# Operand splitting spread over more steps in a spectral FNet plus token-mixing MLP kernel

## The chip, the cores and the metric

The kernel runs on one core of one Trainium2 chip. The metric is the device time of one execution in microseconds (us): the median over several runs. A run is profiled besides, and its trace gives, for each instruction, its engine, source line, start and length.

The engines that matter here are TensorE (matrix products into PSUM; in the profile PE, its weight loads PEld), VectorE (DVE), ScalarE (ACT), GpSimd (POOL) and SyncE (SP). The last two only issue DMA transfers here: SP issues loads, POOL issues stores, most of them accumulating ones, which add to what already lies in DRAM.

## The reference

`x` has 2048 tokens (sequence) by 640 channels, in fp32. The output is the sum of `x` and of two branches that both take the layer-normalized `x`.

```python
xn = _layernorm(x)
# branch A: FNet; Cr, Ci are 2048 x 2048, Hr, Hi are 640 x 640 DFT matrices
a = xn @ Hr.T
b = xn @ Hi.T
A = Cr @ a - Ci @ b
# branch B: token mixer, w1 2048 x 1728, w2 1728 x 2048
h = _layernorm(xn)
u = gelu(h.T @ w1 + b1)          # 640 x 1728
B = (u @ w2 + b2).T              # 2048 x 640
out = x + A + B
```

## The kernel before

**Precision.** Each fp32 operand is cut in two: a high part, which ScalarE makes by a copy to the type fp32r (`high`, L110), and a low part, which VectorE makes by subtracting the high part (`low`, L113). A product is then three matmuls (`three`, L121 to L123): high by high, high by low, low by high. A low part always waits for its own high part.

**Fewer products.** All large products use a Strassen-like scheme: of 2 x 2 blocks, seven products of sums of blocks in place of eight. So VectorE also makes sums and differences of operand blocks (`sub`, L116, and the first sum of a row, L654). In the seven-product stages the results of the products are added up where they can be: several products accumulate in one PSUM bank, the bank is read out after each of them, and the reads build up the result in SBUF (a first read by ScalarE, L699; a later one by VectorE, which adds the bank to the tile, L693).

**Steps and turns.** The whole program is one list of steps. A step is one operand (the weights side: cut into high and low by `cut_piece`) and the matmuls that take it. `turn_of(i, ...)` issues, in program order, everything that belongs to turn i: DMA loads, sums, reads of PSUM, the high part of the operand of step i + 2 (`AHEAD` = 2; three buffers), further sums (`extras`), entries of `timed`, a number of jobs, the low part of the operand of step i + 2, more jobs, and last the matmuls of step i. Each engine runs its own instructions in this order; an instruction that waits holds up all that is behind it on its engine. The order is written by hand in this way, no scheduler moves it.

**Jobs.** The other operand of the products (`moving`) is the same for all rows of a stage and is prepared during the stage before, in small jobs from a list, of which each turn takes the next one or two (`do_jobs`). `moving_of` (L535) cuts one group q of such an operand (128 partitions, two rows of 640) into the seven operands of the scheme: four high parts on ScalarE, three of them of two pieces at once, as many low parts on VectorE, and three sums there, the first of two pieces. It returns a first job and four more, which stand as one-element tuples: after a tuple job, a turn takes no further job, and a turn called with `short` takes no tuple job at all.

**The stages,** in order of the steps:

- *Columns*: steps 0 to 15 (`first_columns`), then seven groups of 32 steps (`columns(g, h, c)`, L443): the DFT over the sequence. h is the half of the sequence that is summed over (the first three groups after the first columns have h = 0, the last four h = 1), c one of four column blocks of 512. A step has nine matmuls of 512 columns where a fifth row block rides along, else six, or three where only that block is computed. The results C11, C12, C21, C22 (two tiles each) and the fifth rows F0, F1 are read out of PSUM at their own turns, by `fresh` (ScalarE copies the bank into a new tile `c`, L510) or `more` (VectorE adds the bank to that tile, L517), and stored by POOL (`store_y`; L401 adds to DRAM where h is 1) into `y_part`. Six tiles `c` are taken in turn (`c_tile`). Of the turns in a group, those in `JOBS_AT` take a job; in the second half (from `s_half`, step 112) these jobs are first those for the five channel DFT matrices (`matrices(q)`, L602), which negate a row on ScalarE (L606) and run `moving_of`.
- *Hidden* (from `s_hid`, step 240): eight rows of seven steps, the DFT over the channels with `y_part` as weights.
- *Up 0* and *up 1* (from `s_up`, step 296): 2 x 7 rows of seven steps, w1 with the normalized sequence rows. `rows_again` fetches two rows of x, scales them on ScalarE (`normalize`, L212) and runs `moving_of`. Up 1 adds what up 0 stored, applies gelu on ScalarE, and the result is cut for the down stages (row groups 0 to 3 at once, the others go through DRAM in `part_up` and come back by `hidden_rows`).
- *Down 0* and *down 1* (from `s_down`, step 394): 2 x 8 rows of seven steps, w2 with the gelu results; down 1 runs over the other row groups.

The rows of hidden, up and down all come from `row_steps` (L641). Its seven steps are the products 1, 5, 6, 2, 7, 3, 4, in this order; reads come one turn after their product, so product 7's read stands in the sixth turn. `loads_of` and `sums_of` (L659 to L665) say at which turn, counted from the row's first step, blocks are loaded and summed. `early` holds for rows of 512 columns of weights or fewer (up and down), and not for hidden.

**How many jobs a turn takes** is set in the last loop (L878 to L887). In up and down, `LONG_AT` lists for each stage the turns of a period that may take a tuple job; the rest are `short`:

```python
LONG_AT = (
    ((1, 3, 6, 8, 10, 13, 15, 17), 21), ((1, 3, 6, 8, 10, 11, 13), 14), ((1, 3, 4), 7),
)
```

Of the kernel before, what the change touches and what calls it, by code (L numbers as in the profile page):

```python
# [23 lines left out]
NF2 = NFB // 2  # L24
# [24 lines left out]
    ((1, 3, 6, 8, 10, 13, 15, 17), 21), ((1, 3, 6, 8, 10, 11, 13), 14), ((1, 3, 4), 7),  # L49
# [4 lines left out]
def fnet_plus_mixer(  # L54
# [60 lines left out]
    def sub(to, a, b):  # L115
        nc.vector.tensor_sub(to, a, b)  # L116
# [273 lines left out]
    c_turn = [3]  # L390
# [52 lines left out]
    def columns(g, h, c):  # L443
# [71 lines left out]
        def more(name, at, key, e, then):  # L515
            def run():
                nc.vector.tensor_add(cs[name, e], banks[key, e], cs[name, e])  # L517
                store_y(h, *then, cs[name, e])
            reads[s0 + at].append(run)

        for e in range(2):
            fresh("C11", 4, "z", e)
            more("C11", 11 + e, "w", e, (0, c, e))
            fresh("C22", 16, "y", e)
            fresh("C12", 20, "z", e)
            more("C12", 28 + e, "y", e, (1, c, e))
            more("C22", 26 + e, "z", e, (1, c, 2 + e))
            fresh("C21", 32, "z", e, (0, c, 2 + e))
# [6 lines left out]
    def moving_of(stage, q, tag, v):  # L535
# [13 lines left out]
        def hi(i, src, n=1):  # L549
            high(moving[stage, q][:, 0, slice(i, i + n) if n > 1 else i, :], src)  # L550
# [6 lines left out]
        def job1():  # L557
            lo(0, piece(0, 0))

            of = v().rearrange("p m (n d) -> p (m n) d", n=2)  # L560
            sub(of[:, 0:2, :], of[:, 1:4:2, :], of[:, 0:2, :])
            hi(3, both(0), 2)

        def job2():
            lo(1, both(1), 2)
            sub(piece(1, 1), piece(1, 1), piece(0, 0))

        def job3():
            lo(3, both(0), 2)
            sub(piece(1, 0), piece(1, 0), piece(1, 1))  # L570
            hi(5, both(1), 2)

        def job4():
            lo(5, both(1), 2)

        return [job0] + [(f,) for f in (job1, job2, job3, job4)]
# [46 lines left out]
    def hidden_rows(q, at):  # L623
        get, _, rest = from_place(at, lambda v: nc.sync.dma_start(v, part_up[4 + q]), [], "down1", q, f"slab{q}")
        return [get] + [None] * 3 + rest
# [15 lines left out]
    def row_steps(stage, nq, load_piece, at, end, bias=(None, None), base=None, earliest=0, each=None):  # L641
# [9 lines left out]
        def first_sum():  # L651
# [9 lines left out]
        sums_of = {  # L661
            -2 if early else -1: (first_sum,),
            0: (lambda: sub(raw["s"], raw["s"], raw["A11"]), lambda: sub(raw["A21"], raw["A11"], raw["A21"])),
            2: (lambda: sub(raw["A12"], raw["A12"], raw["s"]),),
        }  # L665
# [62 lines left out]
    def up(stage, r, at):  # L728
# [3 lines left out]
        def end(c):  # L732
# [17 lines left out]
            timed[e + 5].append(lambda: gelu(0))  # L750
            timed[e + 6].append(lambda: gelu(1))
            if r < 4:
                timed[e + 6].append(lambda: jobs.extend(moving_of("down0", r, f"slab{4 + r}", lambda: c)))
            else:
                timed[e + 7].append(lambda: nc.gpsimd.dma_start(part_up[r], c))

        s0 = row_steps(f"up{stage}", 4, load_piece, at, end)
# [54 lines left out]
    for q in range(4):  # L812
        get, changes, rest = rows_again(0, q, "v")
        timed[s_hid + 4].append(lambda js=[get, None, None] + changes + rest: jobs.extend(js))
# [16 lines left out]
    for q in range(3):  # L831
        timed[s_down + 14 + 7 * q].append(lambda q=q: jobs.extend(hidden_rows(q, ("x0", "v")[q % 2])))
# [44 lines left out]
    with tc.manual_schedule():  # L877
        for i in range(by_hand, len(steps) + 1):  # L878
            n_jobs = (1, i < BLOCK)
            if BLOCK <= i < s_hid - 6:  # L880
                n_jobs = [(i - BLOCK) % GROUP in at for at in JOBS_AT[i >= s_half]]
            short = False
            if i >= s_up:
                at, of = LONG_AT[min((i - s_up) // (7 * NF2), 2)]
                short = (i - s_up) % of not in at
                n_jobs = (1 + (not short), 0)
# [42 lines left out]
```

## Time and profile before

| what | us |
|---|---|
| median of 3 runs | 896.01 |
| lowest and highest of them | 895.9, 896.72 |
| the profiled execution, whole | 896.53 |
| its span in the trace | 894.6 |

The profiled execution is one more run; its span is the time from its first to its last instruction, and the other 1.9 us lie around it. The clock that TensorE was granted is nine tenths or more in each of the 40 slices of the span. How the views that follow are read:

- The page gives, for each engine, its busy time, the share of the span, and the number of instructions. A line of shares follows the chain of work that ended last back through the program.
- A row of the stretches has: start and end in us from the span's start, length; busy time and count (in brackets) of TensorE's matmuls, its weight loads, VectorE, ScalarE and GpSimd; the granted clock of TensorE (1.00 is full); the busy share of the DMA engines; GB/s.
- A row of the timeline has: start, the time from its start to its end (for xN, of N instructions together) in us, engine, line and operation, tile written <- tiles read, sizes; and in square brackets the idle time of the engine just before, with what ended it.
- A row of waits has: the waiting engine, its tile and line <- what ended the wait; us in all, times, the longest.
- A group of instructions has: line, engine, operation, tiles, count | busy us, mean ns of one | idle us just before them, and what ended it.
- A row of DMA issues has: tile written <- read, queue, count, KB each, median us from issue to landing.

### The profile page before, as it was taken

The numbers are of one execution on the slowest core, as the hardware profiler recorded it, in microseconds if no ns is written. First come the engines' busy times: TensorE is split into PE (matmuls) and PEld (weight loads), VectorE is DVE, ScalarE is ACT, GpSimd is POOL, SyncE is SP. The second block draws the span as 40 slices with busy tenths as digits, with TensorE's granted clock in tenths as the row PEclk, the third lists the DMA queues.
The fourth block names the chain that finished last, engine by engine and source line by source line (L and its number), as shares of the span: only waits on it lengthen the run. The fifth ranks groups of instructions, "written<-read, shape, count | busy, mean of one in ns | idle before, by whom it ended". The sixth has DMA issues, their size and how long they took to land.

```text
span 894.6 us, 13967 instructions
## 1 busy us (share of the span) xinstructions
PE 880.5 (98%) x4964; PEld 798.5 (89%) x4964; DVE 714.8 (80%) x1199; ACT 521.0 (58%) x935; POOL 107.8 (12%) x148
## 2 busy tenths in 40 slices
PE   8999999999999999999999999999999999999998
PEld 5888888888888888888999999999989999999998
DVE  8577888785888888588887867888789877887776
ACT  6446576754666564555555645665576655555553
POOL 0110010101121111112100101000000011111111
PEclk9999999999999999999999999999999999999999
DMA  8941554619284655639576765544545787756875
GB/s 293 320 150 60 175 213 128 237 62 359 38 242 65 176 109 172 151 61 185 126 169 152 163 148 159 198 150 142 143 102 140 184 200 179 171 125 133 162 181 107
DMA packets 82951, 143.81 MB, mean 161 GB/s; under 512 B 8129, under 2 KB 33217, under 8 KB 82625
## 3 DMA queue, kind: packets, MB, share of 16 engines
q1 hardware_dynamic: 64848, 95.72, 33.3%
q0 software_dynamic: 18032, 47.20, 27.0%
q8 instruction: 39, 0.64, 0.3%
q14 instruction: 32, 0.25, 0.1%
HBM read 99.63 MB, written 48.50 MB: 166 GB/s over the span
## 4 chain that ended last, share of the span: by engine, by line
PE 88%; DVE 7%; ACT 2%; issue 2%; DMA 1%; SPq 0%; DVEq 0%; ACTq 0%
PE psum L121 29%; PE psum L123 29%; PE psum L122 29%; DVE piece L113 2%; ACT piece L110 1%; DVE sdown L113 1%; DVE pieces L654 1%; DMA pieces<-y 1%; DVE pair L693 1%; DMA pieces<-in_dft_seq 1%; DVE pair L116 0%; DVE st L165 0%; DVE pairs L116 0%; DVE pieces L116 0%; ACT sdown L110 0%
## 5 line engine op out<-in xcount | busy, mean ns | idle before, releaser
L110 ACT ACTIVATE piece<-pieces 128x512 fp32r<-128x512 f32 (+2 forms) x506 | 317.7, 629 | 244.6 <-PE psum L123 142.5
L113 DVE TENSOR_TENSOR piece<-pieces,piece 128x512 fp32r<-128x512 f32 (+2 forms) x506 | 347.8, 689 | 137.7 <-ACT piece L110 128.6
L121 PE MATMUL psum<-piece,n 128*128 128x512 f32 x584 | 228.4, 391 | 2.5 <-ACT n L110 2.5
L122 PE MATMUL psum<-piece,n 128*128 128x512 f32 x584 | 228.5, 391 | 0.2 <-DVE piece L113 0.2
L123 PE MATMUL psum<-piece,n 128*128 128x512 f32 x584 | 227.4, 391 | 0.0
L121 PEld LDWEIGHTS psum<-piece,n 128*128 128x128 f32 x584 | 109.6, 188 | 27.1 <-ACT n L110 3.8
L122 PEld LDWEIGHTS psum<-piece,n 128*128 128x128 f32 x584 | 109.7, 188 | 26.1 <-DVE piece L113 2.6
L123 PEld LDWEIGHTS psum<-piece,n 128*128 128x128 f32 x584 | 109.7, 188 | 23.2
L121 PE MATMUL psum<-sup,piece 128*128 128x320 f32 x392 | 121.5, 310 | 2.2 <-DVE pair L693 1.6
L121 PE MATMUL psum<-sdown,piece 128*128 128x320 f32 x392 | 121.2, 309 | 1.9 <-DVE pair L693 1.7
L123 PE MATMUL psum<-sup,piece 128*128 128x320 f32 x392 | 121.4, 310 | 0.9 <-DVE piece L113 0.9
L123 PE MATMUL psum<-sdown,piece 128*128 128x320 f32 x392 | 121.1, 309 | 0.0
L122 PE MATMUL psum<-sdown,piece 128*128 128x320 f32 x392 | 121.0, 309 | 0.0
L122 PE MATMUL psum<-sup,piece 128*128 128x320 f32 x392 | 121.0, 309 | 0.0
L116 DVE TENSOR_TENSOR pieces<-pieces 128x512 f32<-128x512 f32 (+3 forms) x142 | 109.6, 794 | 2.6
L121 PE MATMUL psum<-shid,piece 128*128 128x320 f32 x280 | 87.0, 311 | 1.2 <-ACT pair L699 1.2
L123 PE MATMUL psum<-shid,piece 128*128 128x320 f32 x280 | 86.8, 310 | 0.3 <-DVE piece L113 0.3
L122 PE MATMUL psum<-shid,piece 128*128 128x320 f32 x280 | 86.5, 309 | 0.0
L121 PEld LDWEIGHTS psum<-sup,piece 128*128 128x128 f32 x392 | 73.6, 188 | 3.5 <-ACT pair L741 1.4
L121 PEld LDWEIGHTS psum<-sdown,piece 128*128 128x128 f32 x392 | 73.6, 188 | 2.6 <-issue 1.8
L123 PEld LDWEIGHTS psum<-sup,piece 128*128 128x128 f32 x392 | 73.6, 188 | 1.4 <-DVE piece L113 1.1
L122 PEld LDWEIGHTS psum<-sup,piece 128*128 128x128 f32 x392 | 73.6, 188 | 0.0
(93 smaller groups left out, 966.1 us busy)
## 6 DMA issues: line engine op xcount, KB each, us to landing
pieces<-in_dft_seq SPq DMA_DIRECT2D x128, 256.0 KB, 5.1
pieces<-in_w SPq DMA_DIRECT2D x88, 256.0 KB, 3.0
y<-c POOLq DMA_DIRECT2D x80, 256.0 KB, 6.0
out<-pair POOLq DMA_DIRECT2D x38, 320.0 KB, 5.7
pieces<-y SPq DMA_DIRECT2D x32, 320.0 KB, 4.9
pieces<-in_w SPq DMA_DIRECT2D x32, 192.0 KB, 2.9
out<-in_x SPq DMA_DIRECT2D x16, 320.0 KB, 6.9
up<-pair POOLq DMA_DIRECT2D x8, 640.0 KB, 4.0
```

The lines of the kernel that those rows point to most:

```text
L110: nc.scalar.activation(hi, src, AF.Copy)
L113: nc.vector.tensor_sub(lo, src, hi.bitcast(F32))
L116: nc.vector.tensor_sub(to, a, b)
L121: nc.tensor.matmul(psum, wh, mh, start=first, stop=False, skip_group_check=True)
L122: nc.tensor.matmul(psum, wh, ml, start=False, stop=False, skip_group_check=True)
L123: nc.tensor.matmul(psum, wl, mh, start=False, stop=last, skip_group_check=True)
L654: nc.vector.tensor_add(raw["s"], raw["A21"], raw["A22"])
L693: nc.vector.tensor_add(c, b, c)
```

## The change

It has the following parts.

1. *The jobs of `moving_of`.* The high parts leave the jobs with the sums and become jobs of their own, without a tuple: job 0 (high parts of the first pieces), job 1 in a tuple (a low part and a sum), job 2 (high part), job 3 and job 4 in tuples (low part and sum, each), job 5 (high part), job 6 in a tuple (low part).
2. *Jobs for each turn.* From `s_half` on a turn that takes jobs takes up to two, all of them ahead of the low part of its operand. As a tuple job ends the taking, these two are mostly a high part and the tuple job behind it. Hidden, where each turn took one job before, gets a list of its own in `LONG_AT`: turns 0, 1, 4 and 5 of seven may take a tuple job, the others are `short`. Up and down already had two jobs in a turn that isn't `short` and one in a `short` one, and keep that.
3. *Last column group* (`g == 2 * NC - 2`). C12 and C22 are no longer read twice into one tile with a VectorE add: both reads are ScalarE copies into tiles of their own, and both are stored with accumulation in DRAM. That is four VectorE adds less, four ScalarE copies and four POOL stores more. The turn of the six `c` tiles starts at another place (`c_turn`), so that it comes out right at the end.
4. *Sums of `row_steps`.* In hidden the sum for A21 moves from turn 0 of a row to turn 2, that for A12 from 2 to 3. Up and down keep their turns. With the sums their operands' slots of `raws` come free later.
5. *Up 1.* The two gelus of a row move from five and six turns behind its last step to six and seven; the jobs that cut the row for down 0, and the store of the other rows, to eight. The loads of the first row of up come at `s_up - 4` at the earliest.
6. *Fetches.* The fetch of the first sequence rows for up 0 is put on the job list at turn `s_hid - 1` in place of `s_hid + 4`. The row groups that down 1 takes back from DRAM are fetched by two jobs at `s_down + 7` and `s_down + 9` and one in the list, in place of each at the head of its own jobs at `s_down + 14`, `+ 21` and `+ 28`, and their other jobs all follow from `s_down + 14`.

```diff
 LONG_AT = (
-    ((1, 3, 6, 8, 10, 13, 15, 17), 21), ((1, 3, 6, 8, 10, 11, 13), 14), ((1, 3, 4), 7),
+    ((0, 1, 4, 5), 7), ((1, 3, 6, 8, 10, 13, 15, 17), 21), ((1, 3, 6, 8, 10, 11, 13), 14), ((1, 3, 4), 7),
 )
...
-    c_turn = [3]
+    c_turn = [5]
...
         def more(name, at, key, e, then):
+            if g == 2 * NC - 2 and name != "C11":
+
+                return fresh(name, at, key, e, then)
+
...
-            fresh("C22", 16, "y", e)
-            fresh("C12", 20, "z", e)
+            last = g == 2 * NC - 2
+            fresh("C22", 16, "y", e, (1, c, 2 + e) if last else None)
+            fresh("C12", 20, "z", e, (1, c, e) if last else None)
...
             sub(of[:, 0:2, :], of[:, 1:4:2, :], of[:, 0:2, :])
+
+        def job2():
             hi(3, both(0), 2)
 
-        def job2():
+        def job3():
             lo(1, both(1), 2)
             sub(piece(1, 1), piece(1, 1), piece(0, 0))
 
-        def job3():
+        def job4():
             lo(3, both(0), 2)
             sub(piece(1, 0), piece(1, 0), piece(1, 1))
+
+        def job5():
             hi(5, both(1), 2)
 
-        def job4():
+        def job6():
             lo(5, both(1), 2)
 
-        return [job0] + [(f,) for f in (job1, job2, job3, job4)]
+        return [job0, (job1,), job2, (job3,), (job4,), job5, (job6,)]
...
-        get, _, rest = from_place(at, lambda v: nc.sync.dma_start(v, part_up[4 + q]), [], "down1", q, f"slab{q}")
-        return [get] + [None] * 3 + rest
+        return from_place(at, lambda v: nc.sync.dma_start(v, part_up[4 + q]), [], "down1", q, f"slab{q}")
...
-        sums_of = {
-            -2 if early else -1: (first_sum,),
-            0: (lambda: sub(raw["s"], raw["s"], raw["A11"]), lambda: sub(raw["A21"], raw["A11"], raw["A21"])),
-            2: (lambda: sub(raw["A12"], raw["A12"], raw["s"]),),
-        }
+        sums_of = defaultdict(list)
+        sums_of[-2 if early else -1].append(first_sum)
+        sums_of[0].append(lambda: sub(raw["s"], raw["s"], raw["A11"]))
+        sums_of[0 if early else 2].append(lambda: sub(raw["A21"], raw["A11"], raw["A21"]))
+        sums_of[2 if early else 3].append(lambda: sub(raw["A12"], raw["A12"], raw["s"]))
...
-            timed[e + 5].append(lambda: gelu(0))
-            timed[e + 6].append(lambda: gelu(1))
+            timed[e + 6].append(lambda: gelu(0))
+            timed[e + 7].append(lambda: gelu(1))
             if r < 4:
-                timed[e + 6].append(lambda: jobs.extend(moving_of("down0", r, f"slab{4 + r}", lambda: c)))
+                timed[e + 8].append(lambda: jobs.extend(moving_of("down0", r, f"slab{4 + r}", lambda: c)))
             else:
-                timed[e + 7].append(lambda: nc.gpsimd.dma_start(part_up[r], c))
-
-        s0 = row_steps(f"up{stage}", 4, load_piece, at, end)
+                timed[e + 8].append(lambda: nc.gpsimd.dma_start(part_up[r], c))
+
+        s0 = row_steps(f"up{stage}", 4, load_piece, at, end, earliest=s_up - 4)
...
-        timed[s_hid + 4].append(lambda js=[get, None, None] + changes + rest: jobs.extend(js))
+        timed[s_hid - 1].append(lambda js=[get, None, None] + changes + rest: jobs.extend(js))
...
-    for q in range(3):
-        timed[s_down + 14 + 7 * q].append(lambda q=q: jobs.extend(hidden_rows(q, ("x0", "v")[q % 2])))
+    gets_hid, _, rests_hid = zip(*(hidden_rows(q, ("x0", "v")[q % 2]) for q in range(3)))
+    for q in range(2):
+        timed[s_down + 7 + 2 * q].append(lambda q=q: jobs.append(gets_hid[q]))
+    timed[s_down + 14].append(lambda: jobs.extend(rests_hid[0] + [gets_hid[2]] + rests_hid[1] + rests_hid[2]))
...
-            n_jobs = (1, i < BLOCK)
+            n_jobs, short = (1, i < BLOCK), False
             if BLOCK <= i < s_hid - 6:
                 n_jobs = [(i - BLOCK) % GROUP in at for at in JOBS_AT[i >= s_half]]
-            short = False
-            if i >= s_up:
-                at, of = LONG_AT[min((i - s_up) // (7 * NF2), 2)]
-                short = (i - s_up) % of not in at
-                n_jobs = (1 + (not short), 0)
+            elif i >= s_hid:
+                k = sum(i >= s for s in (s_up, s_up + 7 * NF2, s_down))
+                at, of = LONG_AT[k]
+                short = (i - (s_up if k else s_hid)) % of not in at
+            if i >= s_half:
+                n_jobs = (2 * n_jobs[0] - short, 0)
```

## The prediction

> **What bounds the kernel now.** I read the page first, then busy time by stretches of time cut at the stage borders, then what TensorE waited for.
>
> ```profile
> span 894.6 us, 13967 instructions
> PE 880.5 (98%) x4964; PEld 798.5 (89%) x4964; DVE 714.8 (80%) x1199; ACT 521.0 (58%) x935; POOL 107.8 (12%) x148
> ...
> PE 88%; DVE 7%; ACT 2%; issue 2%; DMA 1%; SPq 0%; DVEq 0%; ACTq 0%
> ```
>
> TensorE is the bound: the change touches no matmul, so it can only win or lose the short holes between matmuls. The stretches show where these are (start:end, length, then per engine busy time and count; PE comes first, the clock is the 1.00 near the end).
>
> ```profile
> 213.29:361.82 148.53, 148.53 (x649) 121.67 (x648) 120.68 (x176) 87.82 (x148) 25.22 (x30) 1.00 0.61 156
> 361.82:411.79 49.97, 49.79 (x218) 40.30 (x216) 37.05 (x53) 27.41 (x46) 8.13 (x10) 1.00 0.56 111
> 411.79:538.30 126.51, 124.97 (x842) 123.32 (x841) 100.38 (x144) 69.91 (x116) 14.99 (x18) 1.00 0.68 152
> 538.30:625.51 87.21, 86.58 (x590) 86.22 (x589) 74.37 (x125) 52.83 (x98) 4.09 (x7) 1.00 0.53 167
> 625.51:715.62 90.11, 87.67 (x591) 86.25 (x589) 77.74 (x130) 59.57 (x107) 6.28 (x8) 1.00 0.56 141
> 715.62:816.75 101.13, 99.24 (x675) 98.54 (x673) 81.61 (x134) 56.65 (x102) 15.31 (x19) 1.00 0.70 164
> 816.75:890.83 74.08, 74.08 (x506) 73.81 (x504) 56.78 (x112) 38.64 (x83) 12.88 (x16) 1.00 0.73 152
> ```
>
> A row also counts one to three matmuls that cross its edge; the code gives 504 in the last stage, which has no hole: 74.08 / 504 = 0.147 us for a 320-column matmul. A 512-column one comes every 0.227 us (six from 247.64 to 249.00 in the rows further down). So the holes are length minus count times pitch: the three column groups 648 x 0.227, hole 1.4; the last group 216, 0.9; the channel DFT (hidden) 840 x 0.147, 3.0; up 0 and up 1 588 each, 0.8 and 3.7; down 0 672, 2.35. Together 12.2 us; all but the first 1.4, 10.8 us, lie in stages that the change wants to help, and that caps its gain at 1.2%.
>
> ```profile
> PE psum L121 <- DVE pair L693: 3.3, 5, 1.6
> ...
> PE psum L121 <- ACT pair L699: 1.2, 2, 0.7
> ```
>
> These waits of TensorE (us, times, longest) say which wait ends last: mostly not the operand, but the read of a product out of PSUM on VectorE (L693), without which the next product cannot be added to that bank. In a row of steps VectorE must read product 7 during the sixth step, and in the up and down stages the next row's first sum stands ahead of that read.
>
> **The part that costs: a high part and its low part in one step.** Today a job is one turn. From the second half of the columns on, a turn now takes two: job 0 (high parts on ScalarE) and job 1 (their low part and a sum on VectorE) fall into the same turn, and VectorE's low part of the step's own operand stands behind them. The nearest rows are matrix 0 in the columns (ScalarE, VectorE, TensorE):
>
> ```profile
> 244.22 0.62 ACT L110 ACTIVATE piece<-pieces 128x512 fp32r<-128x512 f32 x1
> 244.74 0.73 ACT L606 ACTIVATE hids<-hids 128x640 f32<-128x640 f32 x1
> 245.37 1.09 ACT L110 ACTIVATE shid<-hids 128x320 fp32r<-128x320 f32 x2
> 270.53 1.31 ACT L510 ACTIVATE c<-psum 128x512 f32<-128x512 f32 x2 [0.76 <-PE psum L123]
> ...
> 245.86 0.49 DVE L113 TENSOR_TENSOR shid<-hids,shid 128x320 fp32r<-128x320 f32 x1 [0.29 <-ACT shid L110]
> 246.39 0.82 DVE L116 TENSOR_TENSOR hids<-hids 128x640 f32<-128x640 f32 x1
> 247.13 0.69 DVE L113 TENSOR_TENSOR piece<-pieces,piece 128x512 fp32r<-128x512 f32 x1
> 247.73 1.22 DVE L116 TENSOR_TENSOR pieces<-pieces 128x1024 f32<-128x1024 f32 x1
> ...
> 247.64 0.39 PE L121 MATMUL psum<-piece,n 128*128 128x512 f32 x1
> 249.00 0.39 PE L121 MATMUL psum<-piece,n 128*128 128x512 f32 x1
> 273.81 0.39 PE L121 MATMUL psum<-piece,n 128*128 128x512 f32 x1
> ```
>
> On ScalarE the operand's high part starts at 244.22, the negation 0.52 later, the first high part at 245.37; its low part starts at 245.86, the sum 0.53 and the operand's low part 1.27 after that. In the kernel before the operand at 247.13 is the next step's, due by 249.23 (its second matmul). In the changed order it is the one due by 247.64 + 0.23 = 247.87, and it ends at 247.82: just in time. But the low part (0.85 to the next) and sum (0.41) of the next turn now push the following operand to 249.75, 0.5 late, and the one after (behind a sum of 1.22) by 0.4. Matrix 0: 0.9. Matrix 1 starts a turn with two copies out of PSUM and loses 0.3. Matrix 2 is the bad place: its turn holds steps of 2.04 and 0.68 (9 and 3 matmuls), so the operand is due at 273.81 + 0.23 plus that 0.3. There the copies can start at 271.15 and end two spacings of 0.48 later, the operand's high part follows, the negation at 272.65, the first high part ends at 273.74, and by the distances above the operand's low part ends at 275.8: 1.4 late. The 1.22 sum of the same group is then late by another 0.9. Matrix 3 has longer steps: 0.2. Columns in all: +3.7 (bounds: 2.3 if only matrix 2 loses; 9.2 if each cost its 2.3).
>
> In the down stage the kernel before already has this pairing once; it made the largest hole of the run:
>
> ```profile
> 746.67 1.08 ACT L110 ACTIVATE sdown<-pairs 128x320 fp32r<-128x320 f32 x2
> ...
> 747.17 0.49 DVE L113 TENSOR_TENSOR sdown<-pairs,sdown 128x320 fp32r<-128x320 f32 x1 [1.43 <-ACT sdown L110]
> 747.69 0.82 DVE L116 TENSOR_TENSOR pairs<-pairs 128x640 f32<-128x640 f32 x1
> 749.04 0.48 DVE L693 TENSOR_TENSOR pair<-psum,pair 128x320 f32<-128x320 f32 x1
> 749.44 0.82 DVE L113 TENSOR_TENSOR sdown<-pairs,sdown 128x640 fp32r<-128x640 f32 x1
> 750.70 0.69 DVE L113 TENSOR_TENSOR piece<-pieces,piece 128x512 fp32r<-128x512 f32 x1
> 751.30 0.68 DVE L654 TENSOR_TENSOR pieces<-pieces 128x512 f32<-128x512 f32 x1
> 751.90 0.48 DVE L693 TENSOR_TENSOR pair<-psum,pair 128x320 f32<-128x320 f32 x1
> ...
> 752.53 0.38 PE L121 MATMUL psum<-sdown,piece 128*128 128x320 f32 x1 [1.56 <-DVE pair L693]
> ```
>
> VectorE idles 1.43 for the high part in the fourth step of a row, has a read, a low part and a sum in the fifth, and then the first sum and the read that TensorE waits for. The changed order moves row group 0 clear of this (0.2 left), puts group 1 into the same two steps (1.75 again), and starts group 2 in the fifth step, where I work out 0.8 by the same distances, and 0.6 for its last low part. Down 0: 3.35 instead of 2.35, +1.0 (bounds -2.3, all hidden, and +2.9, three full ones).
>
> **The parts that pay.** *Up 1.* Gelu and the split of its row come one and two steps later, and the third high part no longer holds ScalarE up in the same turn. By the same distances the first row group still delays its row's read by 1.2, the next two by 0.3 and 0.15, where 3.5 of the hole's 3.7 was: -1.8 (bounds -3.5 and 0). *Up 0.* One pairing stays in the fourth step, without the third high part: 0.4 of 0.8 stays, -0.4. *Hidden.* The kernel before splits a row group on consecutive turns together with two sums (0.82 each) of one step:
>
> ```profile
> 468.62 5.55 DMA pieces<-y
> ...
> 511.32 0.43 ACT pair L699
> ```
>
> VectorE is then about two steps' slack behind; a slot comes free late, its load lands late (5.55), and ScalarE's copy (L699) is late for TensorE. With jobs in four of seven steps and the sums at their own steps, VectorE's work per step is at most 2.6 against 15 x 0.147 = 2.2 and falls below it at once. I take all 1.7 us of these holes as gone (bounds -1.7 and 0). What moves with it: the sum for A21 goes two steps down, so the slot of A11 comes free 4.4 us later; from there to the next row's first sum are four steps, 8.8 us, for a load of 4.9 (below). If VectorE ran two steps late there, that load would be the wait.
>
> *Border of the columns and hidden.* Four VectorE adds of the last group become ScalarE copies (two take 1.31 above), and four stores more go through POOL. VectorE's backlog there made holes of 1.75 (0.5 in the last group, 1.25 in hidden). In the changed order the low parts of matrix 4 again wait for high parts of their own turn, and ScalarE has four copies more: I get operands late by 0.45 and 0.25 and a read late by 0.2, and 0.3 for what follows: -0.55 (bounds -1.75 and +2). The 0.3 is for the fetch of the first sequence rows, moved up to the border: it waits until matrix 4 leaves its buffer (410.2 by my sums), lands 4.0 later, and the scaling on ScalarE, with the read behind it, starts at 415.2, half a us after that.
>
> ```profile
> pieces<-y SPq DMA_DIRECT2D x32, 320.0 KB, 4.9
> ...
> pair<-in_x SPq DMA_DIRECT2D x14, 320.0 KB, 4.0
> ...
> y<-c POOLq DMA_DIRECT2D x80, 256.0 KB, 6.0
> ```
>
> ```profile
> L401 POOL DMA_DIRECT2D y<-c x40 | 34.4, 935 | 167.8 <-DVE c L517 155.7 <-ACT c L510 11.7 <-issue 0.5
> ```
>
> *Costed at nothing.* The four stores: 4 x 0.94 on an engine that is 12% busy; each adds to a place stored eight to ten steps (over 11 us) before and landed after 6.0; without that distance it would hold the hidden loads. The down rows' fetches, now up to eight steps ahead; the first up load, one step later but still two steps (4.4) ahead of its use; the buffer of the down rows' store, a step later.
>
> **Sum**, against the profiled execution (896.53 with what lies around the span): +3.7 + 1.0 - 1.8 - 0.4 - 1.7 - 0.55 = +0.25, 896.8. That execution is 0.5 above the median 896.01, so on the scale of the runs I say 896.3: no change.
>
> **Rivals.** *Faster: the reads are not late.* If VectorE reaches the fifth step a us earlier than I think, up 1 loses 0.3 and down 0 1.3, and 3.4 us more are won: 892.9. For it: two later row groups of the kernel before do the same work there and lose only some 0.3 each. Against it: the 1.43 us of idleness above comes with the pairing. *Slower: the pairing costs its worst in every column group.* If all four matrices cost 2.3, it is 5.5 more: 901.8. It decides at two steps: a chain from PSUM copies to the operand's low part of 4.3 us is harmless between steps of 2.04 (4.08 + 0.23) and not between 2.04 and 0.68. The order puts only one there, which speaks against it. *Slower: the first sequence rows land late.* At 5.55, as the load above, instead of 4.0, ScalarE and the read behind it are 1.05 later than put in; with the operand behind that read 2 us: 898.3. From 4.7 on it costs. *Slower: the stores.* If POOL could issue none while VectorE runs without a gap,
>
> ```profile
> 403.19 0.60 DVE c L517
> ...
> 409.45 0.41 DVE pair L116
> ```
>
> the three stores ahead of the first hidden result would go out at about 410, take 3 x 0.94 and 6.0, and land at 419, 3 us after ScalarE needs their tile: 899.3. Against it: under that gapless stretch the mean issue of 0.94 is no longer than elsewhere. The Trainium skill, "SBUF — State Buffer", section "SBUF: two separate sides", has this mechanism: VectorE instructions in a two-port mode keep GpSimd from writing a DMA's descriptors, 3100 ns in place of 620. By that the four stores would take five times 0.94; the trace's 0.94 disagrees, so the chance by this rule is small. *The change does not do what it says* holds in one point already: with two jobs a turn, the first and the last high parts are not a step ahead of their low parts.
>
> **Chances.** No change 0.42; faster by late reads gone 0.28; slower 0.30, of which the columns 0.13, the landing 0.14, the stores 0.03. About 0.2%, 1.8 us, is what a measurement here can tell from no change. The bounds above, taken as independent, give some 2.6 us to either side (893.7 to 898.9); I stretch that to take in the rivals at 892.9, 898.3 and 899.3 and leave out the one at 901.8 and what is faster still: 892.8 to 899.4. The middle case alone reaches 894.2 to 897.8.
>
> **What would show it.** Right: the stretch of the three column groups is about 152, with TensorE waiting for VectorE's low part (L113) at three places; hidden falls to some 124; up 1 to 88.3; down 0 is 102, with the largest hole behind the read of the second row group. Wrong: columns still 148.5 (then faster by 3.5), down 0 under 100, or a load of sequence rows in TensorE's waits.

## The result, and the profile after

| | kernel before | changed kernel |
|---|---|---|
| median, us | 896.04 | 900.87 |
| lowest to highest | 895.64 to 896.72 | 900.08 to 901.77 |
| profiled execution, us | 896.53 | 900.08 |
| span in the trace, us | 894.6 | 897.9 |

The ratio of the times is 1.0053, with a 95% interval of 1.004 to 1.0066: the changed kernel is slower by half a per cent. The forecast was no change at 896.3, with a range up to 899.4.

The page of the changed kernel first: its span, and instructions and busy time of the engines.

```profile
span 897.9 us, 13990 instructions
PE 883.2 (98%) x4964; PEld 798.0 (89%) x4964; DVE 709.9 (79%) x1195; ACT 522.0 (58%) x939; POOL 111.5 (12%) x152
```

As the diff says, VectorE has four instructions fewer, ScalarE four more, GpSimd four more, TensorE as many as before. The longer span is therefore again holes between matmuls. The same stretches as before, cut at the starts of the same matmuls (columns as in the rows of the prediction):

```profile
212.65:365.24 152.59, 150.43 (x650) 121.13 (x649) 119.69 (x176) 87.48 (x148) 25.22 (x30) 1.00 0.59 153
365.24:415.44 50.20, 50.11 (x217) 40.32 (x216) 35.96 (x50) 29.23 (x50) 12.10 (x14) 1.00 0.70 128
415.44:540.87 125.43, 124.78 (x841) 123.19 (x840) 97.21 (x143) 69.69 (x116) 14.65 (x17) 1.00 0.65 154
540.87:627.67 86.80, 86.59 (x591) 86.22 (x589) 74.77 (x125) 53.09 (x98) 4.09 (x7) 1.00 0.51 167
627.67:718.24 90.57, 88.00 (x590) 86.25 (x589) 77.84 (x130) 58.34 (x106) 6.30 (x8) 1.00 0.53 140
718.24:820.36 102.12, 99.43 (x675) 98.57 (x674) 81.56 (x134) 57.47 (x103) 15.32 (x19) 1.00 0.66 162
820.36:894.44 74.08, 74.08 (x506) 73.81 (x504) 56.77 (x112) 38.66 (x83) 12.88 (x16) 1.00 0.72 152
```

Length against length: the three column groups +4.06, the last group +0.23, hidden -1.08, up 0 -0.41, up 1 +0.46, down 0 +0.99, down 1 nothing; +4.2 us together. The span grew by 3.3 only, since in this execution TensorE's first step began 0.5 us earlier, the stages before the first of these rows took 0.2 less, and 0.35 less passed behind the last matmul. Of what the prediction would take as signs of being right, two came: 152.6 us for the three column groups and 102.1 for down 0. Two didn't: up 1 took 90.6 in place of 88.3, longer than before, and hidden 125.4 in place of some 124.

### The profile page after: what moved, and what is told of

Its sections match the earlier page's. It is cut to its first block, busy times and chain, and to the rows that moved or that the text cites. A ratio compares the mean times of both kernels' runs of the same rounds, so it can differ in the third digit from the quotient of the medians.

```text
span 897.9 us, 13990 instructions
## 1 busy us (share of the span) xinstructions
PE 883.2 (98%) x4964; PEld 798.0 (89%) x4964; DVE 709.9 (79%) x1195; ACT 522.0 (58%) x939; POOL 111.5 (12%) x152
## 4 chain that ended last, share of the span: by engine, by line
PE 86%; DVE 7%; ACT 3%; issue 2%; DMA 2%; SPq 0%; DVEq 0%; ACTq 0%
PE psum L122 29%; PE psum L121 29%; PE psum L123 28%; DVE piece L113 3%; DMA pieces<-in_dft_seq 1%; ACT piece L110 1%; DVE pieces L116 1%; DVE shid L113 1%; DVE sdown L113 1%; DVE pieces L662 0%; DVE pair L701 0%; DVE pair L116 0%; DVE st L165 0%; ACT sdown L110 0%; DVE pairs L701 0%
```

## The experiments

In all runs but the repeat and the combinations a part of the changed kernel is undone or altered. A hole is a step's time from its first matmul to the next step's, less its matmuls at 0.227 or 0.147 us. By the pairing I mean a high part and the low part made from it in the same turn. Where a run leaves a stage as it is in the changed kernel, the stage has the same length within 0.2 us in all these traces, except hidden and up 0; so the stretches tell more here than the medians, which are given as ratios to the kernel before, run beside them.

**The columns, without the pairing.** The edit gives the channel DFT matrices their old five jobs, one to a turn:

```diff
+        if stage == "hid":
+            return [job0] + [(lambda fs=fs: [f() for f in fs],) for fs in ((job1, job2), (job3,), (job4, job5), (job6,))]
...
-            if i >= s_half:
+            if i >= s_hid:
                 n_jobs = (2 * n_jobs[0] - short, 0)
```

> The changed kernel, but in the columns the matrices are cut as before: high part, low part and sum in the old five jobs, one job to a turn; all else stays changed. Theory (a high part and the low part behind it in one turn cost TensorE the holes): the three column groups from step 112 on, 152.6 us in the changed kernel, fall back to 148.5, and the whole to 900.9 - 4.05 = 896.8. Rival (the columns' holes only move the backlog from the border into the groups): 148.5 in the groups, but 2 us or more come back in the steps 234 to 250, the whole 899 or more.

The ratio was 1.0018 (1.0008 to 1.0028); in its trace the three groups and the last one:

```profile
213.40:361.89 148.49, 148.49 (x649) 121.68 (x648) 120.68 (x176) 87.83 (x148) 25.17 (x30) 1.00 0.61 158
361.89:411.39 49.50, 49.50 (x217) 40.56 (x216) 35.41 (x49) 29.23 (x50) 12.07 (x14) 1.00 0.72 129
```

The 4.1 us are gone, and the last group did not pay for them: it is 0.7 shorter too. The steps 234 to 250, where the rival wanted 2 us more, have 1.8 us of holes in place of 2.1, so the rival falls. What the pairing does can be read off the changed kernel's own timeline, at the place that the prediction called the bad one: VectorE, then TensorE.

```profile
274.16 0.49 DVE L113 TENSOR_TENSOR shid<-hids,shid 128x320 fp32r<-128x320 f32 x1 [1.21 <-ACT shid L110]
274.69 0.82 DVE L116 TENSOR_TENSOR hids<-hids 128x640 f32<-128x640 f32 x1
275.43 0.69 DVE L113 TENSOR_TENSOR piece<-pieces,piece 128x512 fp32r<-128x512 f32 x1
...
276.17 0.50 PE L122 MATMUL psum<-piece,n 128*128 128x512 f32 x1 [1.19 <-DVE piece L113]
```

VectorE idles 1.21 us until ScalarE has the high part, does that job's low part and sum (1.27 from start to start), and only then the operand's low part, for which TensorE then waits 1.19 us.

The whole did not come down to the 896.8 of the theory. The median of this run is 898.5, 2.2 above its profiled execution, and its executions reach from 896.3 to 901.0: some of what the trace shows as won is lost in others.

**The columns, with the high parts really a turn ahead.** The finer jobs stay, but up to turn 233 a turn takes one:

```diff
-            if i >= s_half:
+            if i >= s_hid - 6:
                 n_jobs = (2 * n_jobs[0] - short, 0)
```

> The changed kernel, but up to turn 233 each turn that takes jobs takes one, so that in the columns a matrix's high parts do stand a turn ahead of their low parts. Theory (the loss in the columns is the pairing in one turn, not the cut into more jobs): the three column groups fall from 152.6 to 148.5 or less (the kernel before had 148.5 with low part, sum and next high part in one turn), the whole by 4. Rival (the longer list is what costs, since it leaves jobs for the border): the groups fall, but the last group and the first row of hidden rise by 1 us or more.

The three groups took 148.51 us: no longer than before, and no shorter. The cut into more jobs costs nothing there, the pairing costs all of the 4.1 us. But the ratio was 1.0021 (1.0012 to 1.0031), and its profiled execution shows another hole, at step 241 (ScalarE, then TensorE):

```profile
417.19 0.92 ACT L212 ACTIVATE pair<-pair,again 128x640 f32<-128x640 f32 x1 [1.39 <-DMA pair<-in_x]
418.01 0.42 ACT L707 ACTIVATE pair<-psum 128x320 f32<-128x320 f32 x1
...
418.48 0.42 PE L121 MATMUL psum<-shid,piece 128*128 128x320 f32 x1 [1.69 <-ACT pair L707]
```

The scaling of the first sequence rows waits 1.39 us for their load, ScalarE's read of PSUM stands behind it, and TensorE behind that. This is the prediction's rival of the landing, and not the longer list: the fetch was issued 1.9 us ahead of hidden's first matmul, as in the changed kernel, but its first row took 6.8 us to land in place of 5.3. The profiled execution is also the slowest of this run's twelve, which reach from 896.7 to 900.5.

**Gelu.** Gelu goes back to its old turns, while the jobs that cut its row stay at the eighth:

```diff
-            timed[e + 6].append(lambda: gelu(0))
-            timed[e + 7].append(lambda: gelu(1))
+            timed[e + 5].append(lambda: gelu(0))
+            timed[e + 6].append(lambda: gelu(1))
```

> The changed kernel with gelu back at its old turns (five and six behind the row); the jobs that cut its row stay at the eighth. Theory (gelu now stands among the four PSUM reads and the first cut of ScalarE, and makes its reads and high parts late): the holes before steps 363, 370, 375 and 382 (0.60 + 0.30 + 0.41 + 0.41 = 1.7 us) go, up 1 falls from 90.6 to 88.9, the whole to 899.2. Rival (VectorE's share of the cut is what is late there, gelu is harmless): up 1 stays within 0.3 of 90.6.

Up 1 fell by 2.4 us:

```profile
630.56:718.77 88.21, 86.82 (x590) 86.23 (x589) 77.85 (x130) 59.57 (x107) 6.28 (x8) 1.00 0.57 144
```

The four holes named (in steps 362, 369, 374 and 381) are all gone, and that at 378 is 0.2 smaller. In the changed kernel the first of them looks like this; ScalarE, VectorE and TensorE:

```profile
652.74 0.83 ACT L749 ACTIVATE pairs<-pairs,b_sb 128x640 f32<-128x640 f32 x1
653.48 0.42 ACT L707 ACTIVATE pair<-psum 128x320 f32<-128x320 f32 x1
653.79 0.62 ACT L110 ACTIVATE piece<-pieces 128x512 fp32r<-128x512 f32 x1
654.32 0.82 ACT L749 ACTIVATE pairs<-pairs,b_sb 128x640 f32<-128x640 f32 x1
655.04 0.42 ACT L707 ACTIVATE pair<-psum 128x320 f32<-128x320 f32 x1
655.35 0.62 ACT L110 ACTIVATE piece<-pieces 128x512 fp32r<-128x512 f32 x1
655.87 1.09 ACT L110 ACTIVATE sdown<-pairs 128x320 fp32r<-128x320 f32 x2
...
656.37 0.49 DVE L113 TENSOR_TENSOR sdown<-pairs,sdown 128x320 fp32r<-128x320 f32 x1 [1.23 <-ACT sdown L110]
656.89 0.82 DVE L116 TENSOR_TENSOR pairs<-pairs 128x640 f32<-128x640 f32 x1
657.64 0.68 DVE L113 TENSOR_TENSOR piece<-pieces,piece 128x512 fp32r<-128x512 f32 x1
...
658.38 0.42 PE L123 MATMUL psum<-sup,piece 128*128 128x320 f32 x1 [0.33 <-DVE piece L113]
```

ScalarE has no gap here: two gelus (0.72 to 0.74 each from start to start), the reads of products 4 and 1, which fall in the first turns of a row, two high parts and the cut's first ones stand in one queue. They come late, so VectorE's low part and sum come late, and the operand behind them. At 374 and 381 it is ScalarE's own read of product 1 that is late. At 374, gelu and a high part of the cut run ahead of it:

```profile
681.65 0.82 ACT L749 ACTIVATE pair<-pair,b_sb 128x640 f32<-128x640 f32 x1
682.37 0.72 ACT L110 ACTIVATE sdown<-pair 128x640 fp32r<-128x640 f32 x1
683.00 0.41 ACT L707 ACTIVATE pairs<-psum 128x320 f32<-128x320 f32 x1
...
683.46 0.42 PE L121 MATMUL psum<-sup,piece 128*128 128x320 f32 x1 [0.25 <-ACT pairs L707]
```

Before, the two gelus ran in the last two turns of a row, which have no ScalarE read. Now the second stands in the first turn of a row, which has the read of product 4, just ahead of the read of product 1 and the cut. The whole shows little of the gain: the ratio was 1.0047 (1.0035 to 1.0059). In the profiled execution hidden was 1.1 us and up 0 0.4 us longer than in the changed kernel's first one, though nothing was edited there.

**The first sum behind the reads.**

```diff
-        sums_of[-2 if early else -1].append(first_sum)
+        (extras if early else sums)[s0 - (2 if early else 1)].append(first_sum)
```

> The changed kernel with one instruction moved in up and down: the next row's first sum stands behind the reads of its turn, not ahead of them. Theory (the holes at steps 364, 371, 378 and 420, 427, 434, 5.3 us together, are the read of product 7 behind that sum and a low part): each loses up to the 0.61 us that the sum takes on VectorE, 0.19 where it has no more, 3.2 us in all; up 1 falls to 89.2, down 0 from 102.1 to 100.3, the whole to 897.7. Rival (the sum is then late for its own high part, and the hole moves a step on): no more than 1 us is won.

Ratio 1.0038 (1.0025 to 1.0051). Down 0 fell from 102.12 to 100.15, with holes of 1.12, 0.25 and none where 1.72, 0.85 and 0.59 had been: each lost 0.6. In up 1 the holes at 364, 371 and 378 lost 0.6, 0.2 and 0.6 too, but those at 369, 374 and 381, which belong to gelu, grew from 0.30, 0.41 and 0.41 to 0.81, 0.68 and 1.01, and the stretch stayed at 90.60. So the theory holds in down 0, and the rival in up 1: there the time went to places where TensorE waits for a low part (369) or for ScalarE's reads (374 and 381).

**Down 0's turns.**

```diff
-((1, 3, 4), 7),
+((1, 3), 7),
```

> The changed kernel with one list changed: in the down stages tuple jobs are taken in turns 1 and 3 of a row, not in 1, 3 and 4. Theory (down 0's holes are low parts and sums of a cut in the fourth and fifth step, ahead of the read of product 7): the holes at steps 420, 427 and 434 (1.72 + 0.85 + 0.59) all go, down 0 falls from 102.1 to 98.9, the whole by 3.2. Rival (the first sum ahead of the read is enough for them): 1.5 us or more of them stay.

Ratio 1.0024 (1.0014 to 1.0034), and no hole left in down 0:

```profile
720.31:818.86 98.55, 98.55 (x674) 98.55 (x673) 82.36 (x134) 57.56 (x103) 15.28 (x19) 1.00 0.71 168
```

**Sums in DRAM, undone.** The condition in `more` and `last` are taken out and `c_turn` is [3] again.

> The changed kernel with the last column group's C12 and C22 read and added on VectorE as before (no sums in DRAM there). Theory (the DRAM sums took four reads off a VectorE that was late at the border, as predicted): the holes of steps 238 to 242, 1.0 us in the changed kernel, rise to 1.7 or more, the whole by 0.7 or more. Rival (ScalarE was as late there, since the four reads became its copies): those holes stay within 0.3 of 1.0.

This part paid, and more than forecast: holes of steps 237 to 242 of 3.70 us in place of 1.17, the last group 51.72 long in place of 50.20, the ratio 1.0084 (1.0066 to 1.0101). Of the 2.5 us, 1.0 is step 241, where the load of the first sequence rows was waited for again (0.95 on ScalarE; it took 6.3 us to land); the rest is VectorE's low parts. Without the DRAM sums these steps have larger holes than the 1.77 us of the kernel before, even without that load. That the pairing, which loads the border as well, makes the difference is my reading; no run undoes both.

**The fetch of the first sequence rows, undone.**

```diff
-        timed[s_hid - 1].append(lambda js=[get, None, None] + changes + rest: jobs.extend(js))
+        timed[s_hid + 4].append(lambda js=[get, None, None] + changes + rest: jobs.extend(js))
```

> The changed kernel with the fetch of the first sequence rows, and so all of up 0's jobs, five turns later, as before. Theory (that fetch can land after ScalarE is ready to scale its rows, with a PSUM read behind it: 1.85 us at step 241 in the execution in which it took longest; and VectorE's jobs start while it is still late from the border): the hole at 241 stays under 0.4, those of 245 to 252 (1.2 us) shrink by 0.5 or more. Rival (hidden's sums in the turn of their high part make these holes whatever the jobs): 1.0 or more of the 1.2 stays, or moves on by five steps.

The hole at 241 went; those of 245 to 252 shrank from 1.2 to 0.43, though 0.2 came at step 266. Ratio 1.0041 (1.0026 to 1.0057). The theory holds, and only a small part moved on, as the rival had it.

**Hidden: sums and turns, four cases.** The sums of hidden at their old turns or the changed ones, and one job a turn or the list of turns. The edits are

```diff
-        sums_of[0 if early else 2].append(lambda: sub(raw["A21"], raw["A11"], raw["A21"]))
-        sums_of[2 if early else 3].append(lambda: sub(raw["A12"], raw["A12"], raw["s"]))
+        sums_of[0].append(lambda: sub(raw["A21"], raw["A11"], raw["A21"]))
+        sums_of[2].append(lambda: sub(raw["A12"], raw["A12"], raw["s"]))
...
-                n_jobs = (2 * n_jobs[0] - short, 0)
+                n_jobs, short = ((1, 0), False) if s_hid <= i < s_up else ((2 * n_jobs[0] - short, 0), short)
```

with the first alone,

> The changed kernel with hidden's sums at their old turns (A21 in turn 0, A12 in turn 2). Theory (in the changed kernel a sum stands in the same turn as the high part that reads it, so sum, high part and low part follow one another and VectorE stalls): the holes at steps 245 to 252 (1.2 us) and 272, 273 (0.36) shrink by at least 1 us, hidden falls from 125.4 to 124.4 or less, the whole to 899.8. Rival (two sums in turn 0 are too much for VectorE and made the holes of the kernel before): hidden rises to 126 or more, the whole to 901.5.

the second alone,

> The changed kernel, but in hidden each turn takes one job, as before, in place of two in turns 0, 1, 4 and 5 and one in the others. Theory (the choice of turns is what took away the holes that the kernel before had at steps 269, 271 and 283, 1.7 us): they or others like them come back, the second half of hidden (steps 268 to 295; 0.3 and 0.7 us of holes in the changed kernel's two profiles) rises to 1.5 or more. Rival (the later sums took them away): it stays under 0.8 unless a load of y is waited for.

and both:

> The changed kernel with one job a turn in hidden and hidden's sums at their old turns: of the kernel before, hidden then differs by the finer jobs alone (and by the earlier fetch). Theory (the later sums took the holes away, as in the last run's rival): 1.2 us or more of holes come back in steps 268 to 295, where the kernel before has 1.9 and one job a turn with the later sums none. Rival (the finer jobs alone do it, as a high part stands a turn ahead of its low part): under 0.5 there.

| holes in hidden, us | old sums | later sums |
|---|---|---|
| two jobs in turns 0, 1, 4, 5 | 0.6 | 1.95 and 2.3 |
| one job a turn | none | none |

The upper row varies. Three other runs that leave hidden as in the changed kernel (gelu, the first sum, down 0's turns) have 3.0, 3.2 and 2.2, and the first combination below, with old sums and the list, has 2.3.

Hidden in the second and the third of these runs:

```profile
416.21:539.43 123.22, 123.22 (x842) 123.20 (x840) 97.41 (x143) 70.74 (x116) 14.52 (x17) 1.00 0.69 157
```

```profile
416.46:539.66 123.20, 123.20 (x842) 123.19 (x840) 98.81 (x143) 69.82 (x116) 14.52 (x17) 1.00 0.70 157
```

840 matmuls by 0.147 are 123.5, so there is no hole at all. My theory of the list fell in the second run and that of the later sums in the third: neither took the holes of the kernel before away. What the two runs without a hole share, against the kernel before, is the finer jobs at one a turn, the earlier fetch and the DRAM sums, which relieve the border; but the kernel before had its larger holes some 28 to 42 steps behind the border. Which of these does it isn't told apart. The list of turns gives this back, with either place of the sums. That the later sums make it worse isn't shown, since one program here varies by more than 1 us. What is shown is that the hole at step 245, 0.3 to 0.9 us in the runs that leave hidden and its jobs as changed, goes with any one of three edits: the old sums, the later fetch, or one job a turn. In the changed kernel it looks like this:

```profile
425.93 0.83 DVE L113 TENSOR_TENSOR piece<-pieces,piece 128x640 fp32r<-128x640 f32 x1 [0.81 <-ACT piece L110]
426.68 0.48 DVE L701 TENSOR_TENSOR pair<-psum,pair 128x320 f32<-128x320 f32 x1
427.08 0.48 DVE L113 TENSOR_TENSOR sup<-pair,sup 128x320 fp32r<-128x320 f32 x1
427.59 0.83 DVE L116 TENSOR_TENSOR pair<-pair 128x640 f32<-128x640 f32 x1
428.34 0.82 DVE L113 TENSOR_TENSOR piece<-pieces,piece 128x640 fp32r<-128x640 f32 x1
429.07 0.48 DVE L701 TENSOR_TENSOR pair<-psum,pair 128x320 f32<-128x320 f32 x1
...
429.70 0.39 PE L121 MATMUL psum<-shid,piece 128*128 128x320 f32 x1 [0.44 <-DVE pair L701]
```

VectorE idles 0.81 for a high part that had to wait for a sum of its own turn, then has no gap up to the read at 429.07. The idle time alone doesn't make the hole: with one job a turn, VectorE has one of 0.86 at the same place and then the same instructions up to the read, but it comes there 0.65 us earlier, counted from the step's first matmul, and TensorE doesn't wait. The ratios are 1.0052 (1.0037 to 1.0067) with the old sums, 1.0018 (1.0009 to 1.0028) with one job a turn, 1.0027 (1.0017 to 1.0036) with both. The first shows no gain in the median. Its profiled execution has 1.35 us less in hidden, but is the fastest of six between 899.3 and 904.0. So the list is what cost hidden its gain, by the traces and by the medians; the place of the sums isn't told by either.

**The changed kernel again.**

> The changed kernel again, unaltered, for a second profile beside the others of this call. Theory (the program's order sets the holes; hidden alone varies, since its loads of y land now sooner, now later): all stretches repeat within 0.1 us, but hidden and up 0, which had 125.4 and 86.8, come out between 210.9 and 213.9 together. Rival (the execution as a whole runs slower or faster): the holes in the columns and in down 0 (5.5 and 3.3 us) differ too, by 0.5 us or more.

The median was 903.68, the ratio 1.0073 (1.006 to 1.0086), so the change costs 0.5 to 0.7 per cent. Every stretch repeats within 0.1 us but these two:

```profile
416.16:541.97 125.81, 124.78 (x841) 123.20 (x840) 97.21 (x143) 69.52 (x116) 14.66 (x17) 1.00 0.66 154
541.97:629.91 87.94, 86.59 (x590) 86.21 (x589) 74.84 (x125) 53.09 (x98) 4.09 (x7) 1.00 0.52 165
```

In up 0 the hole is at step 301, 1.51 in place of 0.36, and VectorE shows why: the row's first sum waits for a load of w1, and the read of product 7 stands behind it.

```profile
552.80 0.69 DVE L662 TENSOR_TENSOR pieces<-pieces 128x512 f32<-128x512 f32 x1 [1.06 <-DMA pieces<-in_w]
553.41 0.48 DVE L701 TENSOR_TENSOR pair<-psum,pair 128x320 f32<-128x320 f32 x1
```

In the runs with this order the hole at 301 is 0.36 to 0.41 us where that sum waits for no load, and 0.68 to 1.51 where it does. In the three runs with the first sum behind the reads it is gone; in one of them, the first combination below, the sum waited 0.6 us for its load, and 0.5 us of holes stood at steps 304 and 305.

**The parts that pay, together.** First with hidden's old sums and the list, then with the later sums and one job a turn:

> The parts put together: the changed kernel with the old jobs in the columns, gelu at its old turns, hidden's sums at their old turns, the first sum behind the reads in up and down, and tuple jobs in turns 1 and 3 in down. Theory (each hole has its own cause): holes of 1.4 in the three groups, 0.5 in the last, 1.2 in hidden (0.6 and what the old jobs of matrix 4 leave there), 0.4, 0.6 and 0 behind; 4.1 in place of 12.2 us, the whole 8 us below the kernel before, 888 where that has 896. Rival (a hole that goes shows the next one, since VectorE's work stays the same): no more than 5 us are won, 891 or more.

> As best_a, but hidden with the later sums and one job a turn. Theory (these two together leave hidden without a hole): hidden's 2.3 us of holes in best_a fall to 0.9 or less (what the old jobs of matrix 4 leave at steps 241 to 245), the rest as in best_a; 1.4 us less than best_a's 889.95 beside a kernel before of 896.8, so 888.5, or a ratio of 0.990. Rival (hidden is held by loads of y, which land as they may): hidden stays within 0.7 of 2.3, the ratio at 0.992.

The first took 889.95 us, ratio 0.9919 (0.9907 to 0.9931): 6.8 us below the kernel before, not 8, as hidden kept 2.3 us of holes in place of 1.2 and up 1 1.3 in place of 0.6. The second took 887.72, ratio 0.9898 (0.9883 to 0.9912), as forecast. Both beat both kernels. From the columns to down 0, the second has

```profile
214.32:362.88 148.56, 148.56 (x649) 121.69 (x648) 120.70 (x176) 87.82 (x148) 25.18 (x30) 1.00 0.62 157
362.88:412.39 49.51, 49.51 (x217) 40.56 (x216) 35.41 (x49) 29.22 (x50) 12.07 (x14) 1.00 0.71 130
412.39:536.32 123.93, 123.93 (x842) 123.20 (x840) 97.89 (x144) 70.22 (x116) 14.51 (x17) 1.00 0.69 157
536.32:622.66 86.34, 86.34 (x591) 86.24 (x589) 74.71 (x125) 53.19 (x98) 4.08 (x7) 1.00 0.54 168
622.66:710.40 87.74, 87.11 (x591) 86.24 (x589) 77.80 (x130) 59.12 (x107) 6.28 (x8) 1.00 0.58 145
710.40:808.96 98.56, 98.56 (x675) 98.56 (x673) 82.34 (x134) 56.92 (x102) 15.28 (x19) 1.00 0.72 168
```

that is, holes of 1.5, 0.5, 0.45, none, 1.3 and none, 3.7 us in place of 12.2.

## Why the prediction was wrong

| term | predicted | trace after less trace before |
|---|---|---|
| columns: pairing of high and low part | +3.7 | +4.05 |
| down 0 | +1.0 | +0.98 |
| up 0 | -0.4 | -0.42 |
| border: last group and steps 240 to 242 | -0.55 | -0.58 |
| hidden from step 243 on | -1.7 | -0.28 |
| up 1 | -1.8 | +0.47 |
| sum | +0.25 | +4.22 |

*Up 1* is the step that failed: "Gelu and the split of its row come one and two steps later", costed as gain alone. The move was priced on VectorE, where the cut stands, and not on ScalarE, where it takes the second gelu out of a turn with no read into one that has a read, just ahead of the next read and the cut. Gelu back at its turns gives 2.4 us: up 1 is then 1.9 us shorter than in the kernel before, where the prediction had 1.8, with holes of 1.26 and 0.45 at 364 and 378 where it had 1.2, 0.3 and 0.15 for the three row groups. So the part of the step that was priced came out, and the part put at nothing cost 2.4.

*Hidden* is the other: "I take all 1.7 us of these holes as gone". Those holes, at 269, 271 and 283, did go; but 1.5 us of others came at 245 to 252, 272 and 273, and the prediction put them at nothing. The work per step was held against its length and found small enough; but the list puts two jobs into a turn, and VectorE then runs late. With one job a turn this term would have held. I take it for the same mechanism that I had priced everywhere else, two jobs in one turn, though the trace doesn't show the single step that makes VectorE late. The two empty jobs that give the fetch its time are also taken two to a turn, so the fetch stands one turn ahead of its use and not three. The prediction gave that load a rival of its own, 2 us at a probability of 0.14, and put its landing at 4.0 us. The first row took 5.3 us in the changed kernel's own trace, just in time; the rival struck in two other profiled executions (1.39 and 0.95 us of wait), where it took 6.8 and 6.3.

*Right:* the columns, with their places: predicted 0.5, 0.4, 0.3, 1.4, 0.9 and 0.2, measured 0.52, 0.36, 0.40, 1.48, 0.88 and 0.26 at steps 135, 136, 146, 150, 152 and 173. So are down 0's three holes (1.75, 0.8 and 0.6 against 1.72, 0.85 and 0.59), and the border. Up 0's 0.4 is right for executions whose load of w1 lands in time, as in this one; it was luck that this one did, as the repeat's 1.51 shows. The border's net fits, but the prediction did not say what each part of the change does to it: the DRAM sums are worth at least the 1.5 us of the last group. The stores cost nothing that shows:

```profile
L401 POOL DMA_DIRECT2D y<-c x44 | 38.0, 952 | 166.7 <-DVE c L521 140.2 <-ACT c L510 26.5
```

44 issues of 0.95 us on the mean, where 40 had 0.94. By the Trainium skill ("SBUF — State Buffer", section "SBUF: two separate sides") GpSimd can't write descriptors while VectorE runs an instruction in a two-port mode, and five times the length for a store is an estimate from its 620 and 3100 ns. The prediction says that the trace's 0.94 disagrees with that rule. That says too much: the longest issue of these stores in any trace here is 1.2 us, but the VectorE instructions beside them at the border are all TENSOR_TENSOR, and no run shows that one of these takes such a mode.

None of the rivals was the outcome as it was put: the columns did not cost their worst, and no read came early. That the change does not do what it says, where two jobs fall into one turn, was said of the columns and down; two jobs in a turn are also what cost hidden its gain.

Between the 4.2 us of these stretches and the 4.8 of the medians lies which execution was profiled: that of the changed kernel is 0.8 below its median, that of the kernel before 0.5 above, and the earlier start and end named above work the other way. What makes loads of `y`, x and w1 land later in some executions than in others isn't settled. In the places looked at (steps 241 and 301) it cost TensorE time because the scaling or the sum that waited for the load had a read of PSUM behind it.

## What to carry to other kernels

Price a moved instruction on every engine that it occupies, turn by turn, not by the mean load of the stage: here an engine off the path, 58% busy, cost 2.4 us because gelu was put among its reads and the next cut. A producer and its consumer on different engines belong in different turns, and if a loop then takes two jobs at once, the distance is gone again. Where the order allows it, put what releases a PSUM bank ahead of anything that can wait for a load; in up 1 this alone won nothing, as the holes moved to other steps of the row.

## What the runs showed that I had not expected

How exactly the holes repeat: step 150 has 1.48 to 1.51 us in all ten profiles of kernels with these columns, while hidden and up 0 together vary by more than 1 us with the landing of loads. And that a late queue can use up a gain: moving one sum took 1.4 us off three holes in up 1 and put 1.4 us on three others.
